# Value products of local attention spaced over iterations and added in three steps, pooled scores of two heads issued in turn

## Chip, cores and metric

The kernel runs on one core of a Trainium2 chip. The metric is device time in microseconds (us) of one execution; lower is better. The engines are TensorE (PE; its weight loads PEld), VectorE (DVE), ScalarE (ACT), GpSimd (POOL) and SyncE (SP, which issues DMAs). Each works through its own queue in order; semaphores tie the queues together.

## The reference, cut to what matters

```python
# q, k, v: (4, 8, 576, 64); 2304 tokens of 8 x 64 = 512 channels
q_d, k_d, v_d = (t.reshape(B, H, 144, 4, 64).mean(axis=3) for t in (q, k, v))
out_up = np.repeat(softmax_attention(q_d, k_d, v_d), 4, axis=2)      # pooled attention
mask = np.abs(pos[:, None] - pos[None, :]) < 4                       # 7 keys a query
out_local = softmax(where(mask, scale * q @ k.T, -1e9)) @ v          # local attention
x = (out_up + out_local).transpose(0, 2, 1, 3).reshape(2304, 512)
r = np.maximum(x @ w_in, 0.0)                                        # 512 -> 2048
x = (r * r) @ w_out                                                  # 2048 -> 512
return ((x @ w_a) * (x @ w_b)) @ w_out2                              # 512 -> 1536 -> 512
```

## The kernel before

The work has a startup, a first stage (attention and the first FFN, to about 544 us) and a second stage (the second FFN). The change lies in the startup and the first stage.

**First FFN.** The 2304 tokens are nine tiles of 256 (0 to 8); the hidden width is 16 blocks of 128. One *iteration* is one tile and one block, number `it` = 16 x tile + block. In the main loop an iteration issues, in this order: the events of kind 0 that are booked for it; `Hidden` (12 matmuls, L593, from the tile's input `xx` into one of three PSUM banks `h`); `high` (three ScalarE passes, L601, L602, L604, that make `g`); the events of kind 1; `low` (one DVE subtraction, L607, that reads the bank and completes `g`); and `project` of iteration `it - 2` (12 matmuls, L614, with that `g`). A `Hidden` begins with the tile's first half of channels (`pi` = 0) and goes on with the second (`pi` = 1).

**Local attention.** Tiles 0 and 1 take it from TensorE as blocks (`Block`), in the startup, whose order is a list written out by hand; `Block.values` (L546) is 16 matmuls of 64 columns a call, four calls. From tile 2 on, `Local(i)` does it on DVE and GpSimd: 128 partitions are 64 groups of four tokens and two channel halves, and each holds four heads. Steps by number `k`: `score_mul` (L373, a product of 1792 elements) and `score_sum` (L382, a reduction) for head h at 2h and 2h + 1; softmax at 8 and 9; `value_mul` (L413, again 1792 elements, followed by the GpSimd adds L421 to L424 over the seven keys) at 10 to 13; `transposes(pi)` (four matmuls, L431, of what the adds left, two heads each) at 14 and 17; `assemble(pi)` (DVE L445, ScalarE L450, DVE L451, which make `xx`) one step later. Step k of tile i stands in iteration 16(i - 1) - 3 + k, with -4 instead of -3 for k < 14 and i > 3. `transposes` are of kind 1, all else of kind 0. Products of scores and values share two buffers in turn (`pr`): one is free when the reduction, or the last add, has read it.

**Pooled attention.** `Pooled(b)` does batch b; batches 2 and 3 run in the iterations of tiles 2 and 3, and 4 and 5. Per channel block `ct` (two heads, four blocks, four iterations apart; the first at iteration 32(b - 1) + 7): scores of head 0 and of head 1 one iteration apart (two matmuls each, L254; fp32, so each matmul shows as two records), minima (DVE L265), exponentials (ACT L275), totals (DVE L282, L283), scaling (ACT L290), transposes (L302), copies (ACT L130), values (four matmuls, L316), output copy (ACT L130). The score matmuls of head 0 use array rows 0 to 63, those of head 1 rows 64 to 127; the value matmuls of the two heads use different array columns. Scores, pooled transposes, values and local transposes take their PSUM bank from one pool of three (`ps_a`).

Of the kernel before, what the change touches and what calls it, by code (L numbers as in the profile page):

```python
# [12 lines left out]
ALU = mybir.AluOpType  # L13
# [62 lines left out]
QB = 64  # L76
# [6 lines left out]
def pooled_local_attention_two_ffn(  # L83
# [19 lines left out]
    nc = tc.nc  # L103
# [87 lines left out]
    class Pooled:  # L191
        def __init__(self, b):
            self.b = b
            self.s, self.t, self.aT, self.a, self.den, self.o, self.mx = {}, {}, {}, {}, {}, {}, {}

            self.steps = [(6, 0, lambda: self.signed(nc.scalar))]
            for ct in range(NCT):
                n = 7 + 4 * ct
                for k, takes, fn, args in (
                    (0, 1, self.scores, (0,)), (1, 1, self.scores, (1,)),  # L200
                    (1, 0, self.minima, (0,)), (1, 0, self.exponentials, (0,)),
                    (2, 0, self.minima, (1,)), (2, 0, self.exponentials, (1,)),
                    (3, 0, self.totals, ()), (3, 0, self.normalised, (nc.scalar,)),
                    (4, 1, self.transposes, (0,)), (5, 1, self.transposes, (1,)),
                    (5, 0, self.copies, (0, nc.scalar)), (6, 0, self.copies, (1, nc.scalar)),
                    (7, 1, self.values, ()), (8, 0, self.outputs, (nc.scalar,)),
                ):
                    self.steps.append((n + k, takes, lambda ct=ct, fn=fn, args=args: fn(ct, *args)))

# [13 lines left out]
        def add(self, j):  # L223
            for n in range(2):
                self.add_part(n, j)
# [24 lines left out]
        def scores(self, ct, h2, kind="a"):  # L250
# [59 lines left out]

        def values(self, ct, kind="a"):
            self.o[ct] = o = bank(kind)
            for h2 in range(2):
                for kc in range(2):
                    c = kc * DM + (2 * ct + h2) * D
                    nc.tensor.matmul(  # L316
                        out=o[64 * h2:64 * h2 + 64, :SG],
                        lhsT=self.vd[:, c:c + D],
                        rhs=self.aT[ct, h2][:, kc],
                        start=(kc == 0), stop=(kc == 1),  # L320
                    )
# [27 lines left out]
    class Local:  # L349
        def __init__(self, i):  # L350
            self.i = i
            self.pv = {}
            self.steps = {}
            for h in range(4):
                self.steps[2 * h] = lambda h=h: self.score_mul(h)
                self.steps[2 * h + 1] = lambda h=h: self.score_sum(h)
                self.steps[10 + h] = lambda h=h: self.value_mul(h)
            self.steps[8] = self.softmax_a
            self.steps[9] = self.softmax_b
            for pi, k in enumerate((14, 17)):  # L360
                self.steps[k] = lambda pi=pi: self.transposes(pi)
                self.steps[k + 1] = lambda pi=pi: self.assemble(pi)

        def score_tiles(self):
            self.s = sm.tile([P, FACTOR, 4, WIN], F32, tag="sc", name="sc")
# [44 lines left out]
        def value_mul(self, h):  # L410
            n = 4 * self.i + h
            p = pr.tile([P, FACTOR, WIN, D], F32, tag="p", name="pv")
            nc.vector.tensor_tensor(  # L413
                out=p, in0=window(heads.pop(("v", n))),
                in1=self.s[:, :, h].unsqueeze(3).to_broadcast([P, FACTOR, WIN, D]), op=ALU.mult,
            )
            load_v(n + 2)
            if h % 2 == 0:
                self.x = xr.tile([P, FACTOR, 2, D], F32, tag="x", name="x")
            add = nc.gpsimd.tensor_tensor  # L420
            add(out=p[:, :, 0:3], in0=p[:, :, 0:3], in1=p[:, :, 3:6], op=ALU.add)  # L421
            add(out=p[:, :, 0], in0=p[:, :, 0], in1=p[:, :, 1], op=ALU.add)  # L422
            add(out=p[:, :, 2], in0=p[:, :, 2], in1=p[:, :, 6], op=ALU.add)  # L423
            add(out=self.x[:, :, h % 2], in0=p[:, :, 0], in1=p[:, :, 2], op=ALU.add)  # L424
            self.pv[h // 2] = self.x

        def transposes(self, pi):
# [28 lines left out]
    class Block:  # L456
# [82 lines left out]
        def values(self, cp, kind):  # L539
            self.o[cp] = o = bank(kind)  # L540
            for c in range(2):
                for h2 in range(2):
                    for blk in range(T1 // QB):
                        bp, half = divmod(blk, 2)
                        ct = 2 * cp + c
                        nc.tensor.matmul(  # L546
# [102 lines left out]
    def at_iteration(it, fn, kind=0):  # L649
        events.setdefault(it, ([], [], []))[kind].append(fn)  # L650
# [11 lines left out]
            if b > 1 or k >= F1:  # L662
                at_iteration(start + k, fn, takes)
    for i in range(PE_TILES, NT1):
        for k, fn in sorted(Local(i).steps.items()):
            at_iteration((i - 1) * F1 - (4 if i > PE_TILES + 1 and k < 14 else 3) + k, fn, k in (14, 17))
    for n in range(2):
        at_iteration((PE_TILES - 1) * F1 - 5, lambda n=n: load_qk(4 * PE_TILES + n))
        at_iteration((PE_TILES - 1) * F1 - 2, lambda n=n: load_v(4 * PE_TILES + n))
# [660 lines left out]
```

## Time and profile before

| | us |
|---|---|
| median of three runs | 953.79 (950.99 to 956.82) |
| profiled execution | 949.86 |
| its span | 948.1 |
| TensorE busy | 895.6 (94%) |
| DVE busy | 692.6 (73%) |
| ScalarE busy | 503.4 (53%) |
| GpSimd busy | 391.8 (41%) |

A share of busy time is a mean over stages with different limits. The start of a tile is the start of its first L593: tile 2 at 184.25, tile 3 at 237.17, tile 4 at 290.39, tile 5 at 344.76, tile 6 at 398.00, tile 7 at 446.73, tile 8 at 495.48 us of the span. In a timeline row the first number is the start, the second the length; ends of matmuls are modelled, so lengths overlap with the next row, and pace is read from start to start.

### The profile page before, as it was taken

Reading aid. Unit: us, or ns where it says so; the run is one execution under the profiler, and the core shown is the slowest. Engines: PE = TensorE matmul, PEld = TensorE weight load, DVE = VectorE, ACT = ScalarE, POOL = GpSimd, SP = SyncE. Lnnn points to the kernel's source line nnn. Section 1 sums busy time; section 2 is a strip of 40 time slices with the busy share of each in tenths; the row PEclk is TensorE's granted clock in tenths of the full one; section 3 lists DMA queues with packets and bytes.
Section 4 is the critical chain, followed back from the end, with each engine's and each line's share of the span. In section 5 each row is a group of like instructions: output and inputs, shape, how many; then the busy total and the mean of one; then the engine's idle time right before and its main releaser. Section 6 shows DMA issues by size and latency. Waiting matters only on the chain.

```text
span 948.1 us, 16541 instructions
## 1 busy us (share of the span) xinstructions
PE 895.6 (94%) x6130; PEld 813.0 (86%) x6130; DVE 692.6 (73%) x975; ACT 503.4 (53%) x1280; POOL 391.8 (41%) x352
## 2 busy tenths in 40 slices
PE   3567899999999999999999999999999999999998
PEld 3457799999999899999999987888888888788888
DVE  3687997678778686878747699898977774665451
ACT  3676985345644465443448656655555552464531
POOL 1645525526092804535353536665565450001010
PEclk9958999999999999999999999999999999999999
DMA  9669732742139221232214314875756659999522
GB/s 291 192 193 261 258 110 62 170 123 69 62 96 211 56 82 49 69 89 69 76 58 148 112 60 148 296 258 177 254 199 213 223 189 347 383 408 353 239 99 79
DMA packets 69888, 161.88 MB, mean 171 GB/s; under 512 B 8472, under 2 KB 16920, under 8 KB 69808
## 3 DMA queue, kind: packets, MB, share of 16 engines
q1 hardware_dynamic: 64336, 142.33, 43.9%
q0 software_dynamic: 2880, 10.03, 5.9%
q10 hardware_dynamic: 2592, 8.47, 2.6%
q8 instruction: 48, 0.79, 0.3%
q14 instruction: 32, 0.26, 0.1%
HBM read 115.71 MB, written 45.09 MB: 170 GB/s over the span
## 4 chain that ended last, share of the span: by engine, by line
PE 77%; DVE 7%; POOL 6%; DMA 6%; issue 2%; ACT 2%; ACTq 0%; SPq 0%; DVEq 0%; POOLq 0%
PE bank L925 39%; PE bank L614 17%; PE bank L593 16%; DMA more<-in_qk_p 2%; POOL pv L422 2%; DVE pv L413 2%; DMA qkd<-in_qk_p 2%; POOL pv L421 2%; PE bank L254 1%; DMA raw<-in_w_in 1%; PE bank L316 1%; DMA raw<-in_w_out 1%; DVE xb L785 1%; POOL x L424 1%; POOL pv L423 1%
## 5 line engine op out<-in xcount | busy, mean ns | idle before, releaser
L593 PE MATMUL bank<-xx,w 128*128 128x256 f32 x1728 | 234.7, 286 | 7.5 <-DVE g L607 2.7
L614 PE MATMUL bank<-g,w 128*128 128x256 f32 x1728 | 233.5, 286 | 3.2 <-DVE g L607 3.2
L925 PE MATMUL bank<-xb,wb 128*128 128x512 f32 x1008 | 231.3, 390 | 1.5 <-ACT r L1021 0.8
L593 PEld LDWEIGHTS bank<-xx,w 128*128 128x128 f32 x1728 | 219.6, 194 | 10.8 <-DVE g L607 3.6
L925 PEld LDWEIGHTS bank<-xb,wb 128*128 128x128 f32 x1008 | 188.4, 188 | 42.2 <-DVE r L975 1.9
L614 PEld LDWEIGHTS bank<-g,w 128*128 128x128 f32 x1728 | 216.2, 191 | 8.7 <-issue 3.9
L925 PE MATMUL bank<-op,wo 128*128 128x512 f32 (+1 forms) x648 | 132.1, 366 | 1.6 <-DVE op L785 1.6
L925 PEld LDWEIGHTS bank<-op,wo 128*128 128x128 f32 x648 | 111.9, 189 | 21.8 <-DVE op L785 2.2
L601 ACT ACTIVATE bank<-bank 128x256 f32<-128x256 f32 x144 | 53.1, 369 | 135.8 <-PE bank L593 133.4
L421 POOL TENSOR_TENSOR pv<-pv 128x768 f32<-128x768 f32 x28 | 55.0, 1963 | 168.9 <-DVE pv L413 168.9
L785 POOL TENSOR_TENSOR wb<-raw,wb 128x256 fp32r<-128x256 f32 x96 | 88.3, 941 | 55.8 <-ACT wb L865 49.6
L607 DVE TENSOR_TENSOR g<-bank,g 128x256 fp32r<-128x256 f32 x144 | 59.3, 418 | 66.7 <-ACT g L604 66.1
L413 DVE TENSOR_TENSOR pv<-vt,sc 128x1792 f32<-128x1792 f32 x28 | 81.0, 2899 | 19.1 <-POOL x L424 19.1
L1021 ACT ACTIVATE r<-bank 128x512 f32<-128x512 f32 x72 | 42.8, 595 | 73.4 <-PE bank L925 71.9
L785 DVE TENSOR_TENSOR op<-ys,op 128x512 fp32r<-128x512 f32 x84 | 54.0, 708 | 31.3 <-ACT op L788 31.3
L788 ACT ACTIVATE op<-ys 128x512 fp32r<-128x512 f32 x84 | 47.1, 624 | 26.1 <-PE bank L925 14.6
L373 DVE TENSOR_TENSOR p<-qt,kt 128x1792 f32<-128x1792 f32 x28 | 59.4, 2121 | 0.0
L130 ACT ACTIVATE raw<-raw 128x512 uint32<-128x512 uint32 (+1 forms) x87 | 53.2, 669 | 9.7 <-DMA raw<-in_w_in 7.4
L785 POOL TENSOR_TENSOR wos<-raw,wos 128x256 fp32r<-128x256 f32 x48 | 46.2, 982 | 28.8 <-ACT wos L865 25.7
L604 ACT ACTIVATE g<-bank 128x256 fp32r<-128x256 f32 x144 | 55.3, 384 | 4.6
L422 POOL TENSOR_TENSOR pv<-pv 128x256 f32<-128x256 f32 x28 | 55.5, 1983 | 2.2
L382 DVE TENSOR_REDUCE sc<-p 128x28 f32<-128x1792 f32 x28 | 56.2, 2007 | 0.0
(121 smaller groups left out, 1085.9 us busy)
## 6 DMA issues: line engine op xcount, KB each, us to landing
ys<-y_d SPq DMA_DIRECT2D x42, 512.0 KB, 8.3
y_d<-r SPq DMA_DIRECT2D x72, 256.0 KB, 2.2
wo_d<-wos SPq DMA_DIRECT2D x48, 256.0 KB, 2.2
kt<-in_k_l SPq DMA_DIRECT2D x28, 320.0 KB, 3.7
vt<-in_v_l SPq DMA_DIRECT2D x28, 320.0 KB, 2.8
raw<-in_w_a SPq DMA_DIRECT2D x12, 512.0 KB, 4.6
raw<-in_w_b SPq DMA_DIRECT2D x12, 512.0 KB, 4.4
raw<-in_w_o SPq DMA_DIRECT2D x12, 512.0 KB, 3.7
```

The lines of the kernel that those rows point to most:

```text
L130: engine.activation(out=out, in_=in_, func=AF.Copy, scale=scale)
L373: nc.vector.tensor_tensor(out=self.p, in0=q.unsqueeze(2).to_broadcast([P, FACTOR, WIN, D]), in1=window(k), op=ALU.mult,)
L382: nc.vector.tensor_reduce(out=self.s[:, :, h], in_=self.p, axis=AX.X, op=ALU.add)
L413: nc.vector.tensor_tensor(out=p, in0=window(heads.pop(("v", n))), in1=self.s[:, :, h].unsqueeze(3).to_broadcast([P, FACTOR, WIN, D]), op=A ...
L421: add(out=p[:, :, 0:3], in0=p[:, :, 0:3], in1=p[:, :, 3:6], op=ALU.add)
L422: add(out=p[:, :, 0], in0=p[:, :, 0], in1=p[:, :, 1], op=ALU.add)
L593: nc.tensor.matmul(out=h, lhsT=wi[f].w[:, a, ct * P:(ct + 1) * P], rhs=x_rhs(i, ct, b), start=(n == 0), stop=(n == 3 * NCT - 1),)
L604: nc.scalar.activation(out=self.g[:, 0], in_=h, func=AF.Copy)
L607: nc.vector.tensor_tensor(out=self.g[:, 1], in0=self.h, in1=self.g[:, 0].bitcast(F32), op=ALU.subtract)
L614: nc.tensor.matmul(out=x2[et // 2][:, et % 2 * T1:(et % 2 + 1) * T1], lhsT=wo[f].w[:, a, et * P:(et + 1) * P], rhs=g[:, b], start=(f == 0 ...
L785: engine.tensor_tensor(out=out, in0=in0, in1=in1, op=ALU.subtract)
L925: nc.tensor.matmul(out=out, lhsT=blk[:, a, cols:cols + P], rhs=rhs[b], start=(start and n == 0), stop=(stop and n == 2), skip_group_check= ...
```

## The change

For tiles from 3 on (`early`), the value products stand at steps 10, 12, 14 and 16, the transposes at 15 and 19 and the assemblies at 16 and 20, and all steps of tile i begin `min(i + 1, 6)` iterations ahead of 16(i - 1). The half in a step number only sorts steps of one iteration. For all tiles the seven products are added in three GpSimd operations (768, 512, 256 elements) instead of four (768, 256, 256, 256). For batches 2 and 3 both heads' scores are issued in one step, matmuls of the two heads in turn, into two banks; transposes, copies, values and outputs move one iteration later. In the values of pooled attention and of the blocks the two heads are issued in turn.

```diff
             for ct in range(NCT):
                 n = 7 + 4 * ct
-                for k, takes, fn, args in (
-                    (0, 1, self.scores, (0,)), (1, 1, self.scores, (1,)),
+                scores = (0, 1, self.scores, (0,)), (1, 1, self.scores, (1,))
+                late = 0
+                if b > 1:
+                    scores, late = ((0, 1, self.both_scores, ()),), 1
+                for k, takes, fn, args in scores + (
...
-                    (7, 1, self.values, ()), (8, 0, self.outputs, (nc.scalar,)),
+                    (7 + late, 1, self.values, ()), (8 + late, 0, self.outputs, (nc.scalar,)),
...
+        def both_scores(self, ct):
+            s = [bank("a") for _ in range(2)]
+            for qc in range(2):
+                for h2 in range(2):
+                    lo = 64 * h2
+                    nc.tensor.matmul(
+                        out=s[h2][:KC, qc * SG:(qc + 1) * SG],
+                        lhsT=self.qd[lo:lo + 64, ct * SG + qc * KC:ct * SG + (qc + 1) * KC],
+                        rhs=self.kd[lo:lo + 64, ct * SG:(ct + 1) * SG],
+                        start=True, stop=True,
+                    )
...
-            for h2 in range(2):
-                for kc in range(2):
+            for kc in range(2):
+                for h2 in range(2):
...
+            self.early = i > PE_TILES
...
-                self.steps[10 + h] = lambda h=h: self.value_mul(h)
+                self.steps[10 + (2 * h if self.early else h)] = lambda h=h: self.value_mul(h)
...
+            self.takes = (15, 19) if self.early else (14, 17)
...
-            add(out=p[:, :, 0:3], in0=p[:, :, 0:3], in1=p[:, :, 3:6], op=ALU.add)
-            add(out=p[:, :, 0], in0=p[:, :, 0], in1=p[:, :, 1], op=ALU.add)
-            add(out=p[:, :, 2], in0=p[:, :, 2], in1=p[:, :, 6], op=ALU.add)
-            add(out=self.x[:, :, h % 2], in0=p[:, :, 0], in1=p[:, :, 2], op=ALU.add)
+            add(out=p[:, :, 0:3], in0=p[:, :, 0:3], in1=p[:, :, 4:7], op=ALU.add)
+            add(out=p[:, :, 0:2], in0=p[:, :, 0:2], in1=p[:, :, 2:4], op=ALU.add)
+            add(out=self.x[:, :, h % 2], in0=p[:, :, 0], in1=p[:, :, 1], op=ALU.add)
...
-                for h2 in range(2):
-                    for blk in range(T1 // QB):
+                for blk in range(T1 // QB):
+                    for h2 in range(2):
...
+            lead = min(i + 1, 6) if local.early else 3
+            at_iteration((i - 1) * F1 - lead + int(k), fn, int(k) in local.takes and (k != int(k) or not local.early))
```

The lines of the changed program have other numbers: L435 is L413 of before, L628 L607, L395 L373, L404 L382, L466 L445, L472 L451, L284 L265, L301 and L302 L282 and L283, L335 L316, L272 L254, L452 L431, L614 L593, L635 L614.

DVE's queue at the end of tile 2, iterations 42 to 45. `pv` is a value product, `p` a score product, `xps` and `xx` the assembly, `den` and `mx` the pooled totals and minima, `g` the FFN's L607. Before:

```order
L282 TENSOR_SCALAR den_2466<-den_2466 72x4
L283 RECIPROCAL den_2466<-den_2466 72x4
L413 TENSOR_TENSOR pv_2559<-vt_2471,sc_2078 128x1792
L607 TENSOR_TENSOR g_2582<-bank_2567,g_2582 128x256
L607 TENSOR_TENSOR g_2612<-bank_2597,g_2612 128x256
L265 TENSOR_REDUCE mx_2642<-bank_2619 72x2
L445 TENSOR_TENSOR xps_2622<-xps_2622,o_sb_106 128x512
L451 TENSOR_TENSOR xx_2649<-xps_2622,xx_2649 128x4x2x64
L373 TENSOR_TENSOR p_2652<-qt_2210,kt_2211 128x1792
L607 TENSOR_TENSOR g_2673<-bank_2658,g_2673 128x256
L265 TENSOR_REDUCE mx_2698<-bank_2680 72x2
```

The same place in the changed program:

```order
L302 RECIPROCAL den_2464<-den_2464 72x4
L435 TENSOR_TENSOR pv_2544<-vt_2389,sc_2043 128x1792
L628 TENSOR_TENSOR g_2567<-bank_2552,g_2567 128x256
L395 TENSOR_TENSOR p_2582<-qt_2174,kt_2175 128x1792
L628 TENSOR_TENSOR g_2603<-bank_2588,g_2603 128x256
L284 TENSOR_REDUCE mx_2629<-bank_2605 72x2
L435 TENSOR_TENSOR pv_2635<-vt_2469,sc_2043 128x1792
L466 TENSOR_TENSOR xps_2611<-xps_2611,o_sb_106 128x512
L472 TENSOR_TENSOR xx_2643<-xps_2611,xx_2643 128x4x2x64
L404 TENSOR_REDUCE sc_2646<-p_2582 128x4x7
L628 TENSOR_TENSOR g_2665<-bank_2650,g_2665 128x256
L284 TENSOR_REDUCE mx_2687<-bank_2606 72x2
```

The last two value products of tile 3 now stand among tile 4's first score product and its reduction, with the first assembly behind the fourth.

TensorE's queue in iteration 46 before, where the pooled values of a channel block and the second local transposes of tile 3 stand between a Hidden and a projection:

```order
L593 MATMUL bank_2748<-xx_2120,w_1282 128x256 x6
L316 MATMUL bank_2765<-aT_2640,vd_1977 64x144 x2
L316 MATMUL bank_2765<-aT_2696,vd_1977 64x144 x2
L431 MATMUL xps_2770<-ident_105,x_2518 128x128 x4
L614 MATMUL bank_2269<-g_2673,w_1337 128x256 x6
```

And in iteration 47 of the changed program:

```order
L335 MATMUL bank_2794<-aT_2685,vd_1973 64x144
L335 MATMUL bank_2794<-aT_2732,vd_1973 64x144
L335 MATMUL bank_2794<-aT_2685,vd_1973 64x144
L335 MATMUL bank_2794<-aT_2732,vd_1973 64x144
L272 MATMUL bank_2799<-qkd_1972 72x144
L272 MATMUL bank_2800<-qkd_1972 72x144
L272 MATMUL bank_2799<-qkd_1972 72x144
L272 MATMUL bank_2800<-qkd_1972 72x144
L452 MATMUL xps_2805<-ident_105,x_2548 128x128 x4
```

Values, both heads' scores and the local transposes now stand in one iteration and take four banks of the pool of three; heads alternate.

DVE's queue in tile 6, iterations 102 to 108, before and after; the value products of tile 7 with an L607 after each:

```order
L413 TENSOR_TENSOR pv<-vt,sc 128x1792
L607 TENSOR_TENSOR g<-bank,g 128x256 x3
L445 TENSOR_TENSOR xps<-xps,o_sb 128x512
L451 TENSOR_TENSOR xx<-xps,xx 128x4x2x64
L373 TENSOR_TENSOR p<-qt,kt 128x1792
```

```order
L628 TENSOR_TENSOR g<-bank,g 128x256 x2
L435 TENSOR_TENSOR pv<-vt,sc 128x1792
L466 TENSOR_TENSOR xps<-xps,o_sb 128x512
L472 TENSOR_TENSOR xx<-xps,xx 128x4x2x64
L395 TENSOR_TENSOR p<-qt,kt 128x1792
```

Shown are the fourth product and what follows. Two L607 now lie between products; after the fourth the assembly and tile 8's first score product follow with no L607 between.

## Rows read from the trace of the kernel before

**Rows 1.** Windows of tiles 4 and 6: length; busy us (instructions) by engine; clock; DMA.

```profile
290.39:344.76 54.37, 52.95 (x434) 50.75 (x433) 42.26 (x50) 26.93 (x82) 24.30 (x20) 1.00 0.47 113
398.00:446.73 48.73, 47.19 (x394) 46.99 (x393) 39.71 (x41) 20.03 (x53) 22.57 (x16) 1.00 0.27 78
```

**Rows 2.** TensorE's timeline at the gaps of tiles 4 and 6: start, length, operation, [idle].

```profile
326.69 0.69 PE L302 MATMUL bank<-ident,a 72*72 72x72 f32 x4 [1.38 <-ACT a L290]
...
413.82 1.60 PE L614 MATMUL bank<-g,w 128*128 128x256 f32 x12
...
429.67 1.61 PE L593 MATMUL bank<-xx,w 128*128 128x256 f32 x12
431.11 0.60 PE L431 MATMUL xps<-ident,x 128*128 128x128 f32 x4
431.46 0.36 PE L614 MATMUL bank<-g,w 128*128 128x256 f32 x1
433.37 1.58 PE L614 MATMUL bank<-g,w 128*128 128x256 f32 x11 [1.54 <-DVE g L607]
```

**Rows 3.** DVE's timeline in tile 6.

```profile
415.24 0.42 DVE L607 TENSOR_TENSOR g<-bank,g 128x256 fp32r<-128x256 f32 x1 [1.47 <-ACT g L604]
415.58 2.02 DVE L413 TENSOR_TENSOR pv<-vt,sc 128x1792 f32<-128x1792 f32 x1
...
423.54 3.65 DVE L413 TENSOR_TENSOR pv<-vt,sc 128x1792 f32<-128x1792 f32 x1 [1.80 <-POOL x L424]
...
432.90 1.07 DVE L607 TENSOR_TENSOR g<-bank,g 128x256 fp32r<-128x256 f32 x3
```

**Rows 4.** GpSimd's timeline in tile 6.

```profile
417.68 1.85 POOL L421 TENSOR_TENSOR pv<-pv 128x768 f32<-128x768 f32 x1 [25.58 <-DVE pv L413]
419.60 2.40 POOL L422 TENSOR_TENSOR pv<-pv 128x256 f32<-128x256 f32 x1
421.97 0.73 POOL L423 TENSOR_TENSOR pv<-pv 128x256 f32<-128x256 f32 x1
...
423.46 1.84 POOL L421 TENSOR_TENSOR pv<-pv 128x768 f32<-128x768 f32 x1
```

**Rows 5.** Groups by line and form: count, busy us, mean ns, idle us and releasers.

```profile
L382 DVE TENSOR_REDUCE sc<-p 128x28 f32<-128x1792 f32 x28 | 56.2, 2007 | 0.0
...
L290 ACT ACTIVATE a<-a,den 72x144 f32<-72x144 f32 x48 | 16.0, 404 | 12.0 <-DVE den L283 12.0
...
L979 POOL TENSOR_TENSOR r<-r 128x512 f32<-128x512 f32 x12 | 16.0, 1331 | 48.3 <-DVE r L975 38.7 <-ACT raw L130 8.6 <-PE bank L925 1.0
```

**Rows 6.** TensorE's timeline at small groups; the 37.68 rows from two windows.

```profile
37.68 1.25 PE L254 MATMUL bank<-qkd 64*72 64x144 f32 x8
37.68 2.19 PE L254 MATMUL bank<-qkd 64*72 64x144 f32 x12
...
205.93 0.71 PE L254 MATMUL bank<-qkd 64*72 64x144 f32 x4
206.57 0.51 PE L614 MATMUL bank<-g,w 128*128 128x256 f32 x2
...
230.63 0.72 PE L316 MATMUL bank<-aT,vd 72*64 72x144 f32 x8
```

**Rows 7.** Startup: TensorE's timeline, and a piece of the chain (start, us, what).

```profile
40.68 2.69 PE L546 MATMUL bank<-aTb,vb 70*64 70x64 f32 x64
...
55.00 3.63 DMA raw<-in_w_in
```

**Rows 8.** Timelines of DVE and TensorE where tile 3 starts.

```profile
231.19 2.03 DVE L373 TENSOR_TENSOR p<-qt,kt 128x1792 f32<-128x1792 f32 x1
...
234.08 0.69 DVE L445 TENSOR_TENSOR xps<-xps,o_sb 128x512 f32<-128x512 f32 x1
235.43 0.69 DVE L451 TENSOR_TENSOR xx<-xps,xx 128x512 fp32r<-128x512 f32 x1 [0.66 <-ACT xx L450]
...
237.16 1.60 PE L593 MATMUL bank<-xx,w 128*128 128x256 f32 x12
```

More of the change, by code (lines that the diff above doesn't have):

```diff
@@ L203, in __init__ @@
                     (3, 0, self.totals, ()), (3, 0, self.normalised, (nc.scalar,)),
-                    (4, 1, self.transposes, (0,)), (5, 1, self.transposes, (1,)),
-                    (5, 0, self.copies, (0, nc.scalar)), (6, 0, self.copies, (1, nc.scalar)),
-                    (7, 1, self.values, ()), (8, 0, self.outputs, (nc.scalar,)),
+                    (4 + late, 1, self.transposes, (0,)), (5 + late, 1, self.transposes, (1,)),
+                    (5 + late, 0, self.copies, (0, nc.scalar)), (6 + late, 0, self.copies, (1, nc.scalar)),
+                    (7 + late, 1, self.values, ()), (8 + late, 0, self.outputs, (nc.scalar,)),
                 ):
@@ L260, in scores @@
             self.s[ct, h2] = s[:KC, :2 * SG].rearrange("p (c k) -> p c k", c=2)
+        def both_scores(self, ct):
[10 more added lines that the diff above has]
+            for h2 in range(2):
+                self.s[ct, h2] = s[h2][:KC, :2 * SG].rearrange("p (c k) -> p c k", c=2)
         def minima(self, ct, h2):
@@ L356, in __init__ @@
                 self.steps[2 * h + 1] = lambda h=h: self.score_sum(h)
-                self.steps[10 + h] = lambda h=h: self.value_mul(h)
+                self.steps[10 + (2 * h if self.early else h)] = lambda h=h: self.value_mul(h)
             self.steps[8] = self.softmax_a
             self.steps[9] = self.softmax_b
-            for pi, k in enumerate((14, 17)):
-                self.steps[k] = lambda pi=pi: self.transposes(pi)
-                self.steps[k + 1] = lambda pi=pi: self.assemble(pi)
+            self.takes = (15, 19) if self.early else (14, 17)
+            for pi, k in enumerate(self.takes):
+                self.steps[k + (0.5 if self.early else 0)] = lambda pi=pi: self.transposes(pi)
+                self.steps[k + 1.5 if self.early else k + 1] = lambda pi=pi: self.assemble(pi)
         def score_tiles(self):
@@ L541, in values @@
             for c in range(2):
-                for h2 in range(2):
-                    for blk in range(T1 // QB):
+                for blk in range(T1 // QB):
+                    for h2 in range(2):
                         bp, half = divmod(blk, 2)
@@ L664, in pooled_local_attention_two_ffn @@
     for i in range(PE_TILES, NT1):
-        for k, fn in sorted(Local(i).steps.items()):
-            at_iteration((i - 1) * F1 - (4 if i > PE_TILES + 1 and k < 14 else 3) + k, fn, k in (14, 17))
+        local = Local(i)
+        for k, fn in sorted(local.steps.items()):
+            lead = min(i + 1, 6) if local.early else 3
+            at_iteration((i - 1) * F1 - lead + int(k), fn, int(k) in local.takes and (k != int(k) or not local.early))
     for n in range(2):
```

## The prediction

> **What bounds the kernel now.** I read the windows by tile first. Tile means 256 tokens, sixteen iterations of the first FFN; iteration t is 16 x tile + f. In each, TensorE runs Hidden (12 matmuls, L593) and the projection of two iterations earlier (12 matmuls, L614). Tile 6 lasts 48.73 us with TensorE busy 47.19, tile 4 lasts 54.37 with 52.95 [rows 1]: TensorE is the bound, and what it loses is a gap of 1.4 to 1.5 us in a tile. So a change gains in two ways only: fewer TensorE microseconds, or no gaps.
>
> Then the TensorE timeline around the gaps. A Hidden takes 1.44 us (429.67 to 431.11 [rows 2]). The projection after it starts at 431.46, and its second matmul, due 0.12 later, starts at 433.37: 1.79 us lost to "DVE g L607" [rows 2]. The same pattern stands once more, in tile 7, with 1.78. In tile 4 the transposes L302 come at 326.69 instead of about 325.25, 1.44 lost [rows 2]. The three sum to 5.0 us; between 130 and 545 us no other gap is over 0.5.
>
> Why the DVE was late: its timeline in tile 6. The four value products (L413) stand in four iterations running. One alone takes 2.02; the third waits for GpSimd until 423.54 and then takes 3.65 [rows 3], so does the fourth, and the three L607 that queue behind that run at 432.90 [rows 3]. GpSimd needs 5.8 us for a head (417.68 to 423.46), two iterations of 2.88. Of its adds L422 takes 2.40 where L423 with the same shape takes 0.73 [rows 4]: one of the two engines stands while the other works on SBUF operands (L413 at 3.65 is 2.02 plus the rest of an L421; L422 at 2.40 is 0.73 plus the rest of an L413). Without that, a head's adds take 1.84 + 3 x 0.73 = 4.0.
>
> **The change part by part.**
>
> *Products two iterations apart, from tile 3 on.* 5.76 us now lie between two L413. One that starts at s ends at s + 2.0; its adds end at about s + 6.1. The next finds at most the last add in its way and loses 0.35, not 1.5 to 3.7. An L607 then stands behind one 2 us product, and it may come 4 us late before TensorE waits (a Hidden's L607 ends 1.8 us after it, 413.82 to 415.66 [rows 2, 3], and the projection needs it after four more groups of 1.44). So the three gaps close: -5.0 us. In tile 7 no score products follow, so there it is certain.
>
> *Three adds instead of four.* 768 + 512 + 256 elements against 768 + 3 x 256: the same elements, one instruction less. The 512 add is not in this place now; its bounds are 0.73 and 1.84 [rows 4], and the row nearest to it is GpSimd's 512-element product of 1.33 [rows 5]. Sum 3.9 against 4.0: nothing by itself.
>
> *Scores of two heads in one step (batches 2 and 3, eight steps).* One head's scores are 4 records that hold TensorE from 205.93 to 206.57, 0.64 us. The values are 8 records and take no longer, 0.72 with the modelled end against 0.71 [rows 6], because their two heads use different columns of the array and run side by side. Scores use different rows for the two heads. Do rows run side by side too? At 37.68, at a slower pace, stand twelve records of three heads; the first two heads use different rows. Their eight records take 1.25 us, all twelve 2.19 [rows 6]: two heads in 1.25, the third alone in 0.94. So yes, nearly. Two heads will cost 0.65 instead of 1.28: 8 x 0.64 = -5.1 us, all on the path, since TensorE is the bound there. If only half the pairs overlap, it is -2.5.
>
> *Order inside the pooled values.* The two heads already overlap though they are issued one after the other (8 records in the time of 4). Nothing to win. [...]
>
> *Order inside the block values (startup, L546).* 64 records take 2.69 [rows 7]; there are 128, 5.4 us, and pairing can at most halve them: up to 2.7 us of TensorE. But the startup's chain of waits leaves TensorE and runs through DMAs issued in between, one of 3.63 us [rows 7]. Bounds 0 and -2.7; nearer to nothing, since the DMAs carry the chain: -0.6.
>
> *What moved costs.* Here the change adds waits. (a) In tile 2 (iterations 42 to 48), lead 4 puts tile 3's last two products next to tile 4's first score products, and the second assembly into iteration 48 itself. Now it stands in 47: its L451 ends at 236.12 and tile 3 starts at 237.16 [rows 8]. I walk through it with zero at the start of Hidden 42. DVE: third product 0.8 to 2.8; score product of 43 (2.03 [rows 8]) waits for the 1.84 add and ends at 6.8; the fourth product needs the buffer of the third, whose adds end at 8.9, so it ends at 11.0. Assembly takes 2.04 with ScalarE in the middle (234.08 to 236.12 [rows 8]), to 13.0; then the score sum (2.0 [rows 5]) to 15.0 and L607 of 44 to 15.35. TensorE, with the added small groups, wants the transposes of 45 at 11.7, in a PSUM bank that this assembly leaves only at 13.0: 1.3 lost. Projection 44 gets its L607 in time. DVE stays three to four us behind, and ScalarE with it, since the scaling L290 (4 x 0.40, [rows 5]) and then Hidden 46's reads stand behind the totals: the reads of 47 end at 22.2. In iteration 47 values, two scores and the local transposes want four banks, and there are three: the transposes wait for the output copy of these very values, behind those reads, to 22.5; TensorE wanted them at 20.7: 1.9 lost. Then the assembly of 48 runs after L607 of 47 and a minimum, from 24.1 to 26.1; Hidden 48 wants its second half at 25.1 to 25.2: 0.9 lost. Sum 4.1.
> (b) In tiles 4, 5 and 6 the fourth product, an assembly and tile i+1's first score product stand in one iteration (74, 90, 106): 2.0 + 2.0 + 2.0 us, plus up to 1.3 if an add takes its turn between. With zero at the end of Hidden 105, L607 of 106 ends at 8.5 to 9.85 and projection 106 wants it at 9.2: 0 to 0.65 in tiles 5 and 6. In tile 4 the local transposes of 77 wait for a copy on ScalarE that stands behind the late DVE: 0 to 1.3. I take 0.65 in tile 4 and 0.35 for the rest. Sum of (a) and (b): +5.1, bounds +2 and +9.
>
> Transposes, copies and outputs of batches 2 and 3 one iteration later: the outputs of the last channel block come at 60 and 92, tiles 4 and 6 read them in 63 and 94; free. The value loads on SyncE's queue follow their products, spread out; a load lands within one iteration; free.
>
> **Sum**, against the profiled execution's 949.86 us (span 948.1): -5.0 - 5.1 - 0.6 + 5.1 = -5.6, 944.3 us. The second stage is bound by TensorE too and shifts whole. The median of the three runs is 953.79, 0.41% above the profiled one, so I forecast 953.79 x 944.3 / 949.86 = 948.2.
>
> **The rivals.**
> *The late DVE gives most of it back* (for: (a) is three waits in a row, each fed by the one before; against: TensorE's own waits let the DVE catch up). New waits of 9: net -1.7, 952.1 on the median's scale.
> *The bank wait repeats.* In iteration 47 four users want three banks; if the transposes or values of all eight channel blocks waited as there, 1.9 us, it would be 8 x 1.9 + 2 = 17 us, net +6.5, 960.3: slower. It decides from 1.1 us a block on: 8 x 1.1 + 2 = 10.8 is all that the other terms gain. Against it: without local transposes in that iteration there are three users.
> *Scores don't overlap*: +5.1 on the forecast, -0.5 in all, 953.3. The change would not do what its order says.
> *The startup shortens in full and the DVE keeps up*: -5.0 - 5.1 - 2.7 + 2 = -10.8, 942.9.
> [...]
>
> **How the numbers follow.** Forecast 0.58, given back 0.17, bank waits 0.07, no overlap 0.05, all good 0.11, values 0.02. A measurement of this kernel can tell about 0.5%, 4.8 us, from no change; the forecast's 5.6 (0.6%) is near that, so of its 0.58 I put 0.43 beyond and 0.15 within. Faster by over 0.5%: 0.43 + 0.11 + 0.02 = 0.56. Slower by over 0.5%: 0.07. Within: 0.15 + 0.17 + 0.05 = 0.37. The forecast's own range is -9 to -2; with the runs' spread of about 2 us around their median the range for 8 in 10 is 943 to 953.5.
>
> **What would show it.** L254 in batches 2 and 3: groups of 8 records of about 0.72 (right) or 1.2 us (no overlap). L413: 28 of about 2.0 to 2.4, none of 3.65 from tile 3 on. Gaps of tile 6 and 7 gone: 47 us a tile. New gaps of TensorE at the end of tile 2: before L302 on DVE L451, before L431 on the ScalarE output copy, before L593 on the assembly. Tile 2 (52.9 now) should become about 54 and tile 4 (54.4) about 51.5. L316 groups stay at 0.72. The forecast is wrong if the end of tile 2 loses under 2 or over 7, or if the startup ends more than 2 us off.

## The result and the profile after

| us | before | after |
|---|---|---|
| median beside each other | 955.10 (950.99 to 956.82) | 942.39 (940.53 to 945.97) |
| again, later (runs of the experiments) | 952.17 (949.47 to 957.22) | 944.73 (942.64 to 948.57) |
| profiled execution, span | 949.86, 948.1 | 940.53, 938.7 |
| start of tile 2 | 184.25 | 182.51 |
| tiles 2 to 7 | 311.23 | 303.58 |

The ratio is 0.9891 (95%: 0.986 to 0.9922) in the first comparison and 0.9922 (0.9896 to 0.9947) in the second: faster by about 0.8 to 1.1%. I had forecast 948.2 (943 to 953.5) against 953.79, a gain of 5.6; the first measurement, 942.39, lies just under that range, the second inside it. Each against the kernel before beside it, the gains are 12.7 and 7.4 us; the first ratio would make 943.4 of 953.79.

Of the 9.4 us by which the span shrank, 7.65 lie in tiles 2 to 7 and 1.74 ahead of them; from tile 8 on both take the same. Busy time first, of the whole span: TensorE lost 6.2 us, DVE 24.7, GpSimd 27.6.

```profile
PE 889.4 (95%) x6130; PEld 808.5 (86%) x6130; DVE 667.9 (71%) x975; ACT 502.2 (54%) x1280; POOL 364.2 (39%) x324
```

The windows of tiles 2, 3, 4, 5 and 6 after (columns as in [rows 1], which answer to the third and the fifth):

```profile
182.51:235.61 53.10, 50.77 (x434) 49.38 (x433) 39.33 (x52) 26.34 (x80) 18.81 (x14) 1.00 0.41 100
235.61:288.88 53.27, 52.57 (x451) 50.78 (x449) 38.74 (x49) 26.30 (x82) 18.90 (x14) 1.00 0.36 95
288.88:340.47 51.59, 51.21 (x434) 49.62 (x433) 38.38 (x50) 28.26 (x84) 20.70 (x16) 1.00 0.49 118
340.47:392.23 51.76, 51.76 (x451) 50.58 (x450) 36.57 (x51) 27.52 (x85) 17.09 (x12) 1.00 0.25 70
392.23:439.16 46.93, 46.93 (x395) 46.93 (x393) 35.17 (x41) 19.63 (x52) 18.91 (x12) 1.00 0.28 80
```

Before they took 52.92, 53.22, 54.37, 53.24 and 48.73 (from the starts of the tiles). In tile 6 TensorE is now busy from end to end, as it was in tile 5 before too; tiles 2 and 3 lost their savings to new waits. The groups of the value products and their adds:

```profile
L435 DVE TENSOR_TENSOR pv<-vt,sc 128x1792 f32<-128x1792 f32 x28 | 58.6, 2099 | 3.0 <-POOL x L445 3.0
L443 POOL TENSOR_TENSOR pv<-pv 128x768 f32<-128x768 f32 x28 | 55.0, 1966 | 181.9 <-DVE pv L435 181.9
L444 POOL TENSOR_TENSOR pv<-pv 128x512 f32<-128x512 f32 x28 | 44.5, 1588 | 2.2
L445 POOL TENSOR_TENSOR x<-pv 128x256 f32<-128x256 f32 x28 | 25.9, 924 | 2.2
```

L435 is 2.10 us in the mean (forecast: 2.0 to 2.4), the longest 2.48, with 3.0 us of waits for GpSimd in front of it; before, that group had 2.90 and 19.1, with the products of 3.65 of [rows 3]. TensorE's timeline where the new waits stand, the end of tile 2:

```profile
224.70 0.41 PE L321 MATMUL bank<-ident,a 72*72 72x72 f32 x4 [0.81 <-DVE xx L472]
...
229.31 1.60 PE L614 MATMUL bank<-xx,w 128*128 128x256 f32 x12
230.84 0.71 PE L335 MATMUL bank<-aT,vd 72*64 72x144 f32 x8
231.48 0.71 PE L272 MATMUL bank<-qkd 64*72 64x144 f32 x8
233.72 0.63 PE L452 MATMUL xps<-ident,x 128*128 128x128 f32 x4 [1.52 <-ACT o_sb L130]
234.10 1.67 PE L635 MATMUL bank<-g,w 128*128 128x256 f32 x12
235.61 0.88 PE L614 MATMUL bank<-xx,w 128*128 128x256 f32 x6
236.79 0.39 PE L614 MATMUL bank<-xx,w 128*128 128x256 f32 x1 [0.29 <-ACT xx L471]
237.51 0.86 PE L614 MATMUL bank<-xx,w 128*128 128x256 f32 x5 [0.34 <-DVE xx L472]
```

These are the three that the prediction named: the transposes wait for the assembly, the local transposes for ScalarE's output copy, tile 3's second half for its assembly. What a group of paired scores takes is read at another one, behind which nothing waits: 204.20 to 204.85, 0.64 us.

```profile
204.20 0.71 PE L272 MATMUL bank<-qkd 64*72 64x144 f32 x8
204.85 1.70 PE L635 MATMUL bank<-g,w 128*128 128x256 f32 x12
```

### The profile page after: what moved, and what is told of

Read it like the earlier page. It is cut to its first block, busy times and chain, and to the rows that moved or that the text cites. A ratio compares the mean times of both kernels' runs of the same rounds, so it can differ in the third digit from the quotient of the medians.

```text
span 938.7 us, 16517 instructions
## 1 busy us (share of the span) xinstructions
PE 889.4 (95%) x6130; PEld 808.5 (86%) x6130; DVE 667.9 (71%) x975; ACT 502.2 (54%) x1280; POOL 364.2 (39%) x324
## 4 chain that ended last, share of the span: by engine, by line
PE 79%; DVE 7%; DMA 5%; POOL 3%; ACT 3%; issue 2%; ACTq 0%; SPq 0%; DVEq 0%; POOLq 0%
PE bank L948 39%; PE bank L635 18%; PE bank L614 18%; DMA more<-in_qk_p 2%; DMA qkd<-in_qk_p 1%; DMA raw<-in_w_in 1%; DVE pv L435 1%; DVE xb L808 1%; PE bank L257 1%; PE bank L335 1%; POOL pv L444 1%; PE bank L321 1%; DVE p L395 1%; POOL w L183 1%; ACT a L294 0%
## 5 line engine op out<-in xcount | busy, mean ns | idle before, releaser
L614 PE MATMUL bank<-xx,w 128*128 128x256 f32 x1728 | 235.4, 286 | 7.1 <-DVE xx L596 2.5
L635 PE MATMUL bank<-g,w 128*128 128x256 f32 x1728 | 233.2, 285 | 0.6 <-DVE g L628 0.4
L614 PEld LDWEIGHTS bank<-xx,w 128*128 128x128 f32 x1728 | 219.5, 193 | 11.3 <-DVE xx L596 2.8
L635 PEld LDWEIGHTS bank<-g,w 128*128 128x128 f32 x1728 | 216.2, 191 | 4.1 <-issue 2.5
L628 DVE TENSOR_TENSOR g<-bank,g 128x256 fp32r<-128x256 f32 x144 | 60.0, 420 | 94.5 <-ACT g L625 94.0
L443 POOL TENSOR_TENSOR pv<-pv 128x768 f32<-128x768 f32 x28 | 55.0, 1966 | 181.9 <-DVE pv L435 181.9
L622 ACT ACTIVATE bank<-bank 128x256 f32<-128x256 f32 x144 | 53.1, 369 | 118.5 <-PE bank L614 116.5
L435 DVE TENSOR_TENSOR pv<-vt,sc 128x1792 f32<-128x1792 f32 x28 | 58.6, 2099 | 3.0 <-POOL x L445 3.0
L395 DVE TENSOR_TENSOR p<-qt,kt 128x1792 f32<-128x1792 f32 x28 | 60.2, 2149 | 0.0
L404 DVE TENSOR_REDUCE sc<-p 128x28 f32<-128x1792 f32 x28 | 56.1, 2004 | 0.0
L623 ACT ACTIVATE bank<-bank 128x256 f32<-128x256 f32 x144 | 53.0, 368 | 4.6
```

Source lines behind the costliest of these rows:

```text
L395: nc.vector.tensor_tensor(out=self.p, in0=q.unsqueeze(2).to_broadcast([P, FACTOR, WIN, D]), in1=window(k), op=ALU.mult,)
L404: nc.vector.tensor_reduce(out=self.s[:, :, h], in_=self.p, axis=AX.X, op=ALU.add)
L435: nc.vector.tensor_tensor(out=p, in0=window(heads.pop(("v", n))), in1=self.s[:, :, h].unsqueeze(3).to_broadcast([P, FACTOR, WIN, D]), op=A ...
L443: add(out=p[:, :, 0:3], in0=p[:, :, 0:3], in1=p[:, :, 4:7], op=ALU.add)
L614: nc.tensor.matmul(out=h, lhsT=wi[f].w[:, a, ct * P:(ct + 1) * P], rhs=x_rhs(i, ct, b), start=(n == 0), stop=(n == 3 * NCT - 1),)
L622: nc.scalar.activation(out=h, in_=h, func=AF.Relu)
```

## The experiments

Each kernel ran beside the kernel before. To compare their tiles free of the startup I split the time from the start of tile 2 to that of tile 8 into three columns. **Waits**: what the start-to-start distances of TensorE's records have over 0.12, summed where a distance is over 0.225 us. **Half pace**: the same for matmuls of the FFN in stretches in which the granted clock is 0.50. **Rest**: what remains.

| | start of tile 2 | tiles 2 to 7 | waits | half pace | rest | median, before beside it | ratio (95%) |
|---|---|---|---|---|---|---|---|
| before | 184.25 | 311.23 | 5.65 | 0 | 305.6 | | |
| after | 182.51 | 303.58 | 4.72 | 0 | 298.9 | 942.39, 955.10 | 0.9891 (0.986, 0.9922) |
| e1_pair | 184.39 | 311.81 | 10.42 | 2.15 | 299.2 | 950.74, 951.60 | 0.9993 (0.9969, 1.0017) |
| e2_space | 186.58 | 312.45 | 4.80 | 1.96 | 305.7 | 953.63, 951.60 | 1.0018 (0.9991, 1.0045) |
| e10_both | 186.89 | 304.41 | 5.42 | 0 | 299.0 | 944.23, 951.85 | 0.9914 (0.9888, 0.9941) |
| e4_adds | 188.74 | 312.22 | 5.42 | 0.93 | 305.9 | 954.09, 951.60 | 1.0016 (0.9991, 1.0041) |
| e3_block | 181.18 | 311.30 | 5.72 | 0 | 305.6 | 953.95, 951.60 | 1.0021 (0.9993, 1.0049) |
| a2_after | 189.82 | 303.60 | 4.75 | 0 | 298.9 | 944.73, 952.17 | 0.9922 (0.9896, 0.9947) |
| e9_blockold | 188.27 | 303.59 | 4.74 | 0 | 298.9 | 944.21, 952.17 | 0.9913 (0.9885, 0.994) |
| e5_heads | 183.34 | 303.63 | 4.73 | 0 | 298.9 | 944.17, 951.85 | 0.9913 (0.9883, 0.9942) |
| e6_lead5 | 185.76 | 304.12 | 3.70 | 1.31 | 299.1 | 944.49, 951.85 | 0.9908 (0.9875, 0.9942) |
| e7_shift | 183.84 | 304.71 | 4.37 | 1.11 | 299.2 | 943.70, 951.85 | 0.9905 (0.9879, 0.9932) |
| e11_pairs | 183.93 | 301.91 | 3.06 | 0 | 298.9 | 940.55, 952.17 | 0.9888 (0.9857, 0.9919) |
| e12_lead4 | 182.03 | 304.53 | 5.45 | 0 | 299.1 | 943.87, 952.55 | 0.9913 (0.9882, 0.9943) |

### The pairing alone (e1_pair)

```diff
-                    (0, 1, self.scores, (0,)), (1, 1, self.scores, (1,)),
...
+                    scores, late = ((0, 1, self.both_scores, ()),), 1
...
-                    (4, 1, self.transposes, (0,)), (5, 1, self.transposes, (1,)),
+                    (4 + late, 1, self.transposes, (0,)), (5 + late, 1, self.transposes, (1,)),
...
```

> The kernel before with the pooled part alone: both heads' scores of batches 2 and 3 in one step, heads in turn, and the steps behind them one iteration later. Local attention, adds and value orders are as before. Theory A (a group that is left out saves also what the change to it and away from it costs): tiles 2 to 5 shorten by 8 x 0.82 = 6.6 us. Rival (only the 0.64 us of the score records themselves go, as the prediction had it): 5.1 us. In both the gaps of tiles 6 and 7 (1.79, 1.78) stay and the score groups of 8 records take 0.64 from start to next start. The start of tile 2 stays at 184.3, within the scatter of executions.

Neither size came out: 311.81 us, no gain, ratio 0.9993. The rest fell by 6.3, as theory A said, but the waits grew by 4.8, and the clock fell twice. TensorE at the end of tile 2 (L319 are the pooled transposes, L270 the paired scores, L631 the projection):

```profile
224.21 0.44 PE L319 MATMUL bank<-ident,a 72*72 72x72 f32 x4 [1.61 <-ACT a L292]
...
233.98 0.72 PE L333 MATMUL bank<-aT,vd 72*64 72x144 f32 x8
234.62 0.46 PE L270 MATMUL bank<-qkd 64*72 64x144 f32 x2
236.42 0.68 PE L270 MATMUL bank<-qkd 64*72 64x144 f32 x6 [1.34 <-DVE xx L468]
237.03 2.93 PE L631 MATMUL bank<-g,w 128*128 128x256 f32 x12
239.76 1.90 PE L610 MATMUL bank<-xx,w 128*128 128x256 f32 x12
```

DVE's timeline tells who is late (L430 value product, L624 the FFN's subtraction, L282 the minimum that the exponentials L292 wait for):

```profile
218.64 3.62 DVE L430 TENSOR_TENSOR pv<-vt,sc 128x1792 f32<-128x1792 f32 x1 [1.31 <-POOL x L441]
222.19 0.74 DVE L624 TENSOR_TENSOR g<-bank,g 128x256 fp32r<-128x256 f32 x2
222.85 0.44 DVE L282 TENSOR_REDUCE mx<-bank 72x2 f32<-72x288 f32 x1
```

The four value products in a row are still there, and the minimum queues behind the fourth. The paired scores hold two of the three PSUM banks at once until exponentials have read them, so the next transposes now wait for that minimum. Later the second head's scores find the third bank held by the local transposes until the assembly has read it. Behind that gap a projection takes 2.73 us from start to start instead of 1.44, at half the clock (the granted clock is the last number but two); the second fall stands in tile 4, behind a gap of 2.86 (0.50 from 333 to 336 us):

```profile
237.00:238.00 1.00, 1.00 (x5) 0.97 (x5) 1.00 (x1) 0.00 (x0) 0.00 (x0) 0.52 0.00 0
```

### The spacing alone (e2_space)

```diff
+                self.steps[10 + (2 * h if self.early else h)] = lambda h=h: self.value_mul(h)
...
+            self.takes = (15, 19) if self.early else (14, 17)
...
+            lead = min(i + 1, 6) if local.early else 3
```

> The kernel before with the local part alone: products two iterations apart and the longer lead from tile 3 on; four adds, scores one head at a time. Both theories: gaps of tiles 4, 6 and 7 close, 5 to 5.7 us in all. Theory A (new waits come of the late DVE and would be there without the pairing): end of tile 2 and starts of tiles 3 and 4 lose about 3 to 4.6 us, net -1 to -2.5. Rival (the new waits need both parts, because four users meet at three PSUM banks only with the pooled steps one iteration later): waits of 1 to 2, net -3.5 to -4.5.

Tiles 6 and 7 became 46.93 as in the changed kernel: the gaps there are gone, so theory A's first half holds. New waits stood without the pairing, 3.7 us at the full clock as theory A said, but not all at the same places: at the end of tile 2 only 0.53 is lost where the changed kernel loses 2.66 (0.97 and 1.69), so those do need the pairing, and at the start of tile 3 more is lost. The total rose by 1.2. At the start of tile 3 (L596 is Hidden, L254 one head's scores, L617 the projection):

```profile
239.56 0.88 PE L596 MATMUL bank<-xx,w 128*128 128x256 f32 x6
241.83 0.39 PE L596 MATMUL bank<-xx,w 128*128 128x256 f32 x1 [1.39 <-ACT xx L453]
242.56 0.86 PE L596 MATMUL bank<-xx,w 128*128 128x256 f32 x5 [0.34 <-DVE xx L454]
...
243.83 1.23 PE L254 MATMUL bank<-qkd 64*72 64x144 f32 x4
244.99 2.93 PE L617 MATMUL bank<-g,w 128*128 128x256 f32 x12
```

The same assembly that costs the changed kernel 1.06 us costs 2.15 here (1.55 + 0.61 over the pace), and then the clock goes to half, 0.65 in the microsecond from 243 and 0.50 from 244 to 250:

```profile
243.00:244.00 1.00, 1.00 (x9) 0.81 (x8) 1.00 (x1) 0.51 (x2) 0.00 (x0) 0.65 0.00 0
```

Of the waits in the table 1.1 are distances at that pace, about 3 us for the fall in all. So neither part alone gains anything.

### Both, and nothing else (e10_both)

> The kernel before with both the pairing of the scores (with the steps one iteration later) and the spacing with the longer lead; four adds, and both value orders as before. Theory B, formed from the two runs of one part each (the parts need each other: the pairing alone leaves the late DVE and the gaps it feeds, the spacing alone leaves the separate score groups in front of the waits, and in both the granted clock falls to 0.50 behind the waits): from the start of tile 2 to the start of tile 8 it takes 303.6 us within 1.0, as the changed kernel does, with a clock of 1.00 in tiles 2 to 7; nearly the whole gain, -8 to -10. Rival (the three adds are part of it, since they shorten the burst at the end of tile 2): clock falls once or waits grow, 306 to 309 us, -3 to -6.

304.41: 6.8 of the 7.65 us, ratio 0.9914, clock 1.00 in all tiles. Theory B holds: the two parts need each other, and the three adds with the two value orders bring the last 0.8 (0.7 of it in waits, 5.42 instead of 4.72). The order of the block values has no part in that: without it tiles 2 to 7 take 303.59 (e9_blockold).

### Three adds alone (e4_adds)

```diff
...
-            add(out=p[:, :, 0], in0=p[:, :, 0], in1=p[:, :, 1], op=ALU.add)
-            add(out=p[:, :, 2], in0=p[:, :, 2], in1=p[:, :, 6], op=ALU.add)
...
+            add(out=p[:, :, 0:2], in0=p[:, :, 0:2], in1=p[:, :, 2:4], op=ALU.add)
...
```

> The kernel before with three adds instead of four, nothing else. Theory A: a head's adds take 3.9 us alone instead of 4.0; DVE and GpSimd still hold each other up with four products in a row, the gaps of tiles 4, 6 and 7 stay within 0.5 us of 1.44, 1.79 and 1.78; time the same within 1 us. Rival (one instruction less shortens the stretch in which the two engines shut each other out): GpSimd needs 5.2 instead of 5.8 a head, the gaps shrink by 1 us or more each, net -3.

The gaps of tiles 6 and 7 shrank by 0.26 each, that of tile 2 too; that of tile 4 grew to 1.80, and there the clock fell, to 0.50 from 333 to 335 us (L302 transposes, L613 projection, 2.67 from start to start):

```profile
331.18 0.69 PE L302 MATMUL bank<-ident,a 72*72 72x72 f32 x4 [1.64 <-ACT a L290]
...
333.20 2.84 PE L613 MATMUL bank<-g,w 128*128 128x256 f32 x12
335.87 1.60 PE L592 MATMUL bank<-xx,w 128*128 128x256 f32 x12
```

Theory A holds: no gain of its own.

### The startup (e3_block, e9_blockold, a2_after)

```diff
-                for h2 in range(2):
-                    for blk in range(T1 // QB):
+                for blk in range(T1 // QB):
+                    for h2 in range(2):
```

e3_block is the kernel before with this alone, e9_blockold the changed kernel without it, a2_after the changed kernel once more.

> The kernel before with the heads of the block values in turn, nothing else. Theory A (the order gives the startup's 1.7 us): the two single groups of 32 records shrink and tile 2 starts at 182.5 instead of 184.25. Rival (the startup hangs on DMAs, and executions differ by as much whatever the order): 64 records take 2.0 instead of 2.6, but tile 2 starts within 183.5 to 185. Times: -1.7 or 0 to -0.6.

> The changed kernel with the block values issued head after head as before, nothing else. Theory (execution scatter; the DMAs carry the startup): 64 records take 2.6 instead of 2.0, the start of tile 2 anywhere between 182 and 187, median within 1 us of the changed kernel run beside it. Rival (the order gives the startup's 1.7): median 1.7 to 2.7 us longer than the changed kernel's.

> The changed kernel once more, to see how far its startup differs between executions and as partner of the next run. From the start of tile 2 to that of tile 8 303.6 within 0.3 (all theories); the start of tile 2 somewhere between 181 and 186 if the startup hangs on its DMAs, at 182.5 within 0.5 if the order of the block values had shortened it.

The order does shorten the group, as the lines of a2_after and then of e9_blockold show:

```profile
L567 PE MATMUL bank<-aTb,vb 70*64 70x64 f32 x128 | 6.0, 270 | 1.3 <-ACT a L294 1.3
```

```profile
L567 PE MATMUL bank<-aTb,vb 70*64 70x64 f32 x128 | 7.8, 274 | 0.1
```

But the same changed kernel reached tile 2 at 182.51 in one execution and in a2_after at 189.82. Most of that arose between the starts of tiles 0 and 1: 66.13 to 129.24 in the one, 67.58 to 136.54 in the other. There TensorE stood still in a2_after, and the granted clock was 0.83 from 66 to 131 us where it had been 0.92:

```profile
112.52 0.69 PE L321 MATMUL bank<-ident,a 72*72 72x72 f32 x4 [3.73 <-DVE w L183]
```

L183 makes `w` from weights that come by DMA: on the chain of work that ended last, the transfer `raw<-in_w_in` holds 9.45 us there, 5.93 in the other execution. Why it did isn't shown.

Over all profiles that start lies between 181.18 and 189.82, and the medians show no gain: ratio 1.0021 for the order alone, 944.21 without it against 944.73 with it. e3_block's profile alone would have spoken for the order (181.18); its timed runs don't. The 1.74 us ahead of tile 2 in the result lie within this scatter and aren't shown to be an effect.

### Heads in turn or head after head (e5_heads)

```diff
-            for qc in range(2):
-                for h2 in range(2):
+            for h2 in range(2):
+                for qc in range(2):
```

> The changed kernel with the paired scores of batches 2 and 3 issued head after head (two matmuls of head 0, then two of head 1), otherwise the same. Theory (heads on different rows overlap only when they stand next to each other in the queue, the second matmul of a head doesn't let the next head past): 8 records take 0.9 to 1.28 us instead of 0.64, tiles 2 to 5 get 2 to 5 us longer. Rival (as the pooled values did before the change, heads overlap whatever the order): 0.64 to 0.66, same time within 1 us.

```profile
205.03 0.72 PE L272 MATMUL bank<-qkd 64*72 64x144 f32 x8
205.68 1.70 PE L635 MATMUL bank<-g,w 128*128 128x256 f32 x12
```

0.65 us, and 303.63 in the tiles: the rival was right. What saves time is that both heads stand together; the turn order does nothing. One head's four records alone hold TensorE for 0.64 in the kernel before [rows 6], so in either order the two heads run side by side. How their matmuls start within the 0.65 us this row doesn't tell. In the kernel before, the eight records of the pooled values, queued head after head, start in pairs 0.01 to 0.02 us apart (at 230.63 and 230.65, then at 230.81 and 230.82), while one head's scores start 0.12 to 0.18 apart (205.93, 206.11, 206.24, 206.36). If each pair is one record of either head, which the trace doesn't print, TensorE's matmuls didn't start strictly in the order of its queue there.

### One iteration more of lead (e6_lead5), pooled steps one earlier (e7_shift)

```diff
-            lead = min(i + 1, 6) if local.early else 3
+            lead = min(i + 2, 6) if local.early else 3
```

> The changed kernel with one iteration more of lead for tiles 3 and 4 (5 and 6 instead of 4 and 5). Theory (the waits at the starts of tiles 3 and 4 come of an assembly in the tile's own first iterations): the 1.06 at the start of tile 3 and the 0.58 at that of tile 4 go, net -1 to -2. Rival (the local transposes, now one iteration earlier, hold the third bank when values and both scores want three; as with the pairing alone, where the second head's scores waited 1.50 for the assembly): a wait of 1 to 2 behind the scores at the end of tile 2, 0 to +2, and if the clock falls there +3 to +4.

```diff
-                n = 7 + 4 * ct
+                n = (6 if b == 2 else 7) + 4 * ct
```

> The changed kernel with the pooled steps of batch 2 one iteration earlier (scores at iterations 38, 42, 46 and 50), so that values, both scores and the local transposes no longer stand in one iteration at the end of tile 2. Theory (that wait of 1.60 comes of four users of three banks): it goes, and the transposes' 0.97 as well; the 1.06 at the start of tile 3 stays or grows, since the DVE decides it: net -1 to -2.5. Rival (the late DVE carries all of these waits and only moves them on): the start of tile 3 loses 2 to 3 instead, 0.

Both rivals had the mechanism, but not all of the rest: e6_lead5 lost only 0.5 us in the tiles in spite of the fall of the clock (3 to 4 were expected), and in e7_shift the wait moved ahead of the local transposes, not to the start of tile 3. In e6_lead5 the waits at the starts of tiles 3 and 4 went, and the second head's scores waited 2.01 for the assembly that holds the third bank; the clock fell, to 0.50 from 239 to 242 us:

```profile
235.95 0.46 PE L272 MATMUL bank<-qkd 64*72 64x144 f32 x2
238.26 0.68 PE L272 MATMUL bank<-qkd 64*72 64x144 f32 x6 [1.85 <-DVE xx L472]
238.86 2.86 PE L635 MATMUL bank<-g,w 128*128 128x256 f32 x12
```

In e7_shift the collision went, and the local transposes waited 2.37 for a bank that exponentials free, behind a minimum behind the late DVE; the clock fell again, to 0.50 from 237 to 239 us:

```profile
236.22 0.89 PE L452 MATMUL xps<-ident,x 128*128 128x128 f32 x4 [2.27 <-ACT a L294]
236.77 2.91 PE L635 MATMUL bank<-g,w 128*128 128x256 f32 x12
```

304.12 and 304.71: shifting what waits doesn't help while DVE is late, in these two places at least.

### Another spacing (e11_pairs, e12_lead4)

```diff
+                self.steps[10 + ((0, 1, 3, 4)[h] if i < 5 and self.early else 2 * h if self.early else h)] = lambda h=h: self.value_mul(h)
...
+            self.takes = (15, 19) if i > 4 else (14, 17)
```

> The changed kernel with another spacing of the value products in tiles 3 and 4 alone: steps 10, 11, 13 and 14 instead of 10, 12, 14 and 16, transposes at 14 and 17, assemblies one later; lead as in the changed kernel. Theory (the waits at the ends of tiles 2 and 3, 4.6 us in all, come of the fourth product, an assembly and the next tile's first score product close together on DVE): no such burst is left, the waits shrink to 0 to 2 us, from the start of tile 2 to that of tile 8 it takes 299 to 301.5 us instead of 303.6. Rival (two products in neighbouring iterations shut GpSimd out again, products of 3.65 and adds of 2.40, and the DVE is as late, only two iterations earlier): waits of 3 to 5 at other places, 303 to 305.

301.91, 1.7 us under the changed kernel, with waits of 3.06; medians 940.55 against 944.73 beside it. Theory and rival each have a part. No burst is left at the tile's end, but neighbouring products do shut GpSimd out. DVE, then GpSimd:

```profile
215.38 3.64 DVE L435 TENSOR_TENSOR pv<-vt,sc 128x1792 f32<-128x1792 f32 x1 [0.61 <-POOL x L445]
```

```profile
215.30 1.83 POOL L443 TENSOR_TENSOR pv<-pv 128x768 f32<-128x768 f32 x1
217.22 2.95 POOL L444 TENSOR_TENSOR pv<-pv 128x512 f32<-128x512 f32 x1
```

The product lasts until 219.02, 1.89 us after the end of L443 (217.13), where a product alone takes 2.02. L444, 1.29 us alone (at 224.57 in the changed kernel), lasts until 220.17, 1.15 after the end of the product. So each stood while the other ran, within 0.15 us of the lengths alone. Not every pair of instructions does that: in the changed kernel L444 and L445 ran at 224.57 and 225.93 beside the reduction L404 (224.47, 2.01 us) and took 1.29 and 0.73, and L404 takes 1.98 to 2.01 in all its 28 instances. "Works on SBUF operands", as the prediction has it, is therefore too wide; the rows here show it for the products and the adds.

e12_lead4 is that kernel with a lead of 4 in tile 4 and its local transposes one step later.

> The run before last with the other spacing (steps 10, 11, 13 and 14 in tiles 3 and 4), and in tile 4 a lead of 4 instead of 5 with the local transposes one step later (15 and 18). Theory (of the 3.1 us of waits that are left there, 1.1 and 0.6 come of tile 4's first score product, 3.4 us long beside the last adds, in front of the minima that two pooled transposes wait for, and 0.9 of transposes that come before the last add of their product): these three shrink to 0.7 together or less, from the start of tile 2 to that of tile 8 299.5 to 300.5 instead of 301.9. Rival (the last product of tile 4 now falls together with the first score product of tile 5, so the wait only moves into the end of tile 4): 301.5 to 303.

Tile 2 gained 1.1 us more (51.89), and tiles 3 and 4 lost 3.7: tile 4's last two products and tile 5's first score product now follow each other, the latter waits for its buffer and is then shut out itself (3.65 us, 2.01 alone), and the FFN subtraction behind it lets TensorE wait 2.00; tile 4's start loses 1.6 more. That is the rival's mechanism, at a higher price than it named (304.53). DVE, then TensorE:

```profile
273.25 3.65 DVE L395 TENSOR_TENSOR p<-qt,kt 128x1792 f32<-128x1792 f32 x1 [1.98 <-POOL x L445]
```

```profile
275.16 0.28 PE L635 MATMUL bank<-g,w 128*128 128x256 f32 x1
277.29 1.57 PE L635 MATMUL bank<-g,w 128*128 128x256 f32 x11 [1.84 <-DVE g L628]
```

e11_pairs is the fastest kernel of this study. Its lead over the changed kernel rests on 1.7 us in the tiles; the intervals of the two ratios overlap.

## Why the prediction was right or wrong

By its own terms, all in tiles 2 to 7: -5.65 (gaps) - 6.7 (scores) + 4.72 (new waits) = -7.6, and 7.65 were measured. Forecast were -5.0, -5.1 and +5.1 with -0.6 in the startup.

- **Gaps: right, a little small.** The three closed. Two stalls under 0.5 us, which I had left out (0.37 in tile 2, 0.19 in tile 4), closed with them.
- **Scores of two heads: right mechanism, term too small.** The rest column is 305.7 in the mean of the four kernels without the pairing and 299.0 in that of the ten with it: 6.7 us, as between before and after, 0.84 for each of eight groups. I had priced a group by [rows 6] from its start to the next start, 0.64. A group also delays its neighbours: 229.31 to 230.84 is 1.53 for a Hidden ahead of a small group, where 1.44 is the pace, and 234.10 to 235.61 is 1.51 for the projection behind one. That is 0.16 more, 0.80 of the 0.84: what the change between the two kinds of matmul costs goes with the group.
- **Value orders: right.** The pooled values take 0.64 (230.84 to 231.48), against 0.65 before (230.63 to 231.28), and e5_heads shows that the scores wouldn't need their turn order either: eight records of neighbouring heads take 0.64 in turn and 0.65 head after head.
- **Startup: not shown.** I took 0.6 us; the medians show none of it, and two executions of one kernel differ by 7.3 us there. For the same reason the sign that I set, a startup over 2 us off, could tell nothing.
- **Three adds: nothing alone, right,** with L444 at 1.29 alone against the estimate of 1.33. Beside the others they, the order in the pooled values, or both bring the last 0.8 us, which I didn't see.
- **New waits: right in place and size at the end of tile 2.** Forecast 1.3, 1.9 and 0.9; measured 0.97, 1.69 and 1.06. In tile 4 the place was wrong: none at the local transposes of iteration 77, but 0.58 at the tile's start and 0.43 in two smaller ones near it. Tiles 5 and 6 show none where I put 0.35.
- **The rivals fell.** Scores overlap; the bank wait stands in one iteration and not in eight; the late DVE gives back 4.7 and not 9; the pooled values keep their pace; the startup shows no gain. The 0.02 for values, which is in the sum of the chances for faster, stood for a gain from their new order; no run shows one, the group takes 0.64 after and 0.65 before.

The step that failed in the reasoning, though not in the sum, is that I priced the two parts one by one, -5.0 for the gaps and -5.1 for the scores. e1_pair and e2_space say that each alone is worth nothing (ratios 0.9993 and 1.0018), and e10_both that together they are worth 6.8 us. The pairing takes two of three banks at once, and without the spacing a late DVE frees them late; the spacing leaves a wait at tile 3's start that is longer without the pairing. Both ended in falls of the clock, which I had not listed as a risk at all; they are seen in one profiled execution of each.

The first comparison's 1.1% is more than the tiles give, 7.65 of 950 or 0.8%, which is what the second shows; the difference is within the intervals, and the scatter of the startup is large enough for it.

## What to carry to other kernels

Price a small group of matmuls by what the iteration around it gets shorter, not by the group's own length: here 0.84 instead of 0.64 us. Two edits that feed each other's slack are tested together and apart, since one that is worth nothing alone can be half of the gain. Where the startup scatters from execution to execution, compare kernels from a tile start behind it, and read the waits from start-to-start distances.

## What the runs showed of the hardware

From the start of tile 2 to that of tile 8 the granted clock is 1.00 in the kernels before and after; in the startup, from 50 to 66 us, it is 0.52 and 0.50. In five of the other kernels it falls to 0.50 in tiles 2 to 7 behind some gaps of TensorE: 1.50 and 2.86 (e1_pair), 1.55 and 0.61 (e2_space), 1.80 (e4_adds), 2.01 (e6_lead5), 2.37 (e7_shift). It didn't fall behind 1.78 and 1.78 (before), 1.81 and 1.80 (e1_pair, tiles 6 and 7), 1.77 ahead of pooled transposes (e1_pair), 1.69 and then 0.45 and 0.61 (after), 2.00 (e12_lead4). None fell behind a lone gap within a projection (1.78 to 2.00); beside small groups (transposes, scores) some did and some didn't. Length alone doesn't decide, and the runs don't settle what does. One fall cost 0.9 to 2.0 us in the FFN's matmuls.
